# Layer 0 of a four-layer attention and GLU kernel: chunk 1 transposed by TensorE too, layer norms first, some work on GpSimd

## Chip, cores, metric

One NeuronCore of one Trainium2 chip. The metric is device time of one execution in microseconds (us), lower is better. Executions of one kernel mostly agree within 1%. Times were taken on several chips, always with runs of the kernel before on the same chip, so kernels are compared by their ratio to the kernel before.

## The reference

```python
x = x + A(layernorm(x))    # layers 0 and 2: 16 heads of 28, keys at distance 0, 2, .. 14, softmax, @ wo
x = x + B(layernorm(x))    # layers 1 and 3: h = (x @ w_gate) * (x @ w_up); h @ w_down
# x: 1 x 2048 x 448 bf16; w_gate, w_up: 448 x 1792; w_down: 1792 x 448
```

## The kernel before

Tokens are split by parity (each parity attends only to itself) and cut into 4 chunks of 512. x stays in SBUF. A chunk's path in an attention layer: layer norm on VectorE, a transpose of each normalised 128-row block into `xnTa`, QK and V matmuls, then, per query block of 120, scores, Exp, a mask product, denominators and A·V, a reciprocal as Ln and Exp, a product, and finally the `wo` matmul and the residual add. The GLU layers read the transposed `xnTb`.

The Python code contains a list scheduler. Every operation has a priority, dependencies and an assumed duration. The scheduler plays time forward with those assumed durations and so fixes, before anything runs, the order of instructions on each engine. On the chip each engine takes its instructions in that order and waits on semaphores. **A wrong assumed duration costs nothing by itself, but an instruction placed too early holds up everything behind it.**

```python
PE_T = ("00",)      # (layer, chunk) transposed by TensorE instead of by DMA
WARM = 20           # dummy matmuls at the start
SEQ = "A00 A01 B10 A02 B11 A03 B12 A20 ...".split()      # A/B, layer, chunk

    # weights of the GLU layers: issued from GpSimd once chunk 2 of x has landed
    xl = [("x", -1, 11)]
    for nm, Wt, src, ... in (("wg", WG, ...), ("wu", WU, ...)):
        plain_dma("pool", Wt[:, c, :], src[...], (nm, c), f"d_{nm}", deps=xl, lat=12000.0, prio=-30)   # ... WT likewise
    plain_dma("pool", WD[:], ..., "wd", "d_wd", deps=xl, lat=16000.0, prio=-29)
    # ...
    def ln_chunk(li, j, prio):
        # per block: bn_stats, bn_aggr (VectorE); per half or chunk: Ln, Exp (ScalarE) -> rstd
        for B in range(4 * j, 4 * j + 4):
            slot, prev = ring("xn", ...)          # 6 slots, given out in the order of ln_chunk calls;
            sc.add("dve", ... ("xn", li, B), 325.0, deps=[("rstd", li, B), ..., prev])    # prev: the slot's last transpose
            if not by_pe:
                sc.add("sp", one(lambda E: E.dma_start_transpose(X[:, :, c0:c0 + 128], xn_sb[:, slot, :]), ("T", li, B)),
                       1270.0, deps=[("xn", li, B)] + war + ..., lat=1500.0, ...)
            else:                                  # four 128x128 TensorE transposes into PSUM, one eviction by ScalarE or VectorE
    # ...
    for n, job in enumerate(SEQ):
        ln_chunk(li, j, -30.0 + n * 0.5)           # so the ring goes 00, 01, 10, 02, ...
        if job[0] == "A": a_chunk(li, j, prio)     # qk_chunk, v_group, attn_front/back, y_block
        else: b_chunk(li, j, nb, prio)
```

The softmax here doesn't subtract the row's maximum and nothing guards it: scores larger than these inputs give would overflow.

## Time and profile before

| | before |
|---|---|
| time, median (range) | 457.93 us (455.83 to 459.05) |
| span in the profile | 453.6 us |
| busy: TensorE, VectorE, ScalarE, GpSimd | 421.1, 244.1, 222.6, 11.1 us |

The median is of the three runs known before the change.

In the profile PE is TensorE's matmuls, DVE VectorE, ACT ScalarE, POOL GpSimd, SP the queue that issues the transposes; L507 is a line of the program. These are lines of the page's strip: the span in 40 slices of 11.3 us, each digit the busy share in tenths, PEclk the recorded TensorE clock in tenths of full speed.

```profile
PE   5814877999999999999999999999999999999997
PEclk9765995999999999999999999999999999999999
DMA  8896002410002210010020310020020201001001
```

From the eighth slice on TensorE is full: it bounds the kernel there. Everything to be had lies in the first seven slices. The same in numbers, from the table of windows: stretch in us, its length, then busy time (and instruction count) of PE, its weight loads, DVE, ACT and POOL, the recorded clock, the DMA share and GB/s.

```profile
24.00:39.70 15.70, 0.40 (x19) 0.26 (x18) 0.03 (x1) 2.64 (x3) 0.00 (x0) 0.58 1.04 210
39.70:44.00 4.30, 4.30 (x13) 1.06 (x13) 2.25 (x4) 0.00 (x0) 0.00 (x0) 0.54 0.30 61
44.00:68.00 24.00, 18.96 (x312) 8.37 (x311) 18.98 (x35) 21.82 (x33) 0.00 (x0) 0.99 0.01 2
68.00:78.00 10.00, 7.53 (x72) 2.97 (x71) 8.08 (x21) 4.42 (x9) 0.00 (x0) 0.51 0.27 54
78.00:453.60 375.60, 372.50 (x2713) 152.47 (x2710) 200.68 (x382) 180.80 (x281) 0.00 (x0) 1.00 0.11 23
```

TensorE did 0.40 us of work in the 15.7 us from 24 us on, while the DMA engines were full. The list of waits (who waited for whom, total us, times, longest us) names the wait:

```profile
DVE xn_sb L479 <- DMA xnTa<-xn_sb: 21.0, 1, 21.0
PE ps L507 <- DMA xnTa<-xn_sb: 15.3, 1, 15.3
```

L507 is here the QK matmul of chunk 1; L479 is a normalise, held up because its slot of the ring (the six buffers of `xn_sb`, which hold normalised blocks until they are transposed) is still being read by a transpose. The DMA queues in the window from 20 to 26 us (queue, packets, MB, share of the 16 engines) show why the transposes are late; q0 carries the weights that GpSimd issued, q1 the transposes:

```profile
q0 software_dynamic: 173, 0.96, 79.8%
q1 hardware_dynamic: 320, 0.08, 14.7%
```

The SP queue's timeline (start, length, what) has the third oddity: chunk 2's last two transposes of `xnTa` come behind four for layer 1 (`xnTb`), since the ring gives chunk (1,0) its slots before chunk (0,2).

```profile
14.58 28.02 SPq L484 DMA_TRANSPOSE xnTa<-xn_sb  x6
68.61 5.12 SPq L484 DMA_TRANSPOSE xnTb<-xn_sb  x4
77.67 2.50 SPq L484 DMA_TRANSPOSE xnTa<-xn_sb  x2
```

### The profile page before, as it was taken

Reading aid. Unit: us, or ns where it says so; the run is one execution under the profiler, and the core shown is the slowest. Engines: PE = TensorE matmul, PEld = TensorE weight load, DVE = VectorE, ACT = ScalarE, POOL = GpSimd, SP = SyncE. Lnnn points to the kernel's source line nnn. Section 1 sums busy time; section 2 is a strip of 40 time slices with the busy share of each in tenths; the row PEclk is TensorE's granted clock in tenths of the full one; section 3 lists DMA queues with packets and bytes.
Section 4 is the critical chain, followed back from the end, with each engine's and each line's share of the span. In section 5 each row is a group of like instructions: output and inputs, shape, how many; then the busy total and the mean of one; then the engine's idle time right before and its main releaser. Section 6 shows DMA issues by size and latency. Waiting matters only on the chain.

```text
span 453.6 us, 7740 instructions
## 1 busy us (share of the span) xinstructions
PE 421.1 (93%) x3204; PEld 173.1 (38%) x3204; DVE 244.1 (54%) x484; ACT 222.6 (49%) x350; POOL 11.1 (2%) x30
## 2 busy tenths in 40 slices
PE   5814877999999999999999999999999999999997
PEld 3201333333444333433344334433344334334333
DVE  6602788434769727761389616861477542442432
ACT  4530993577666567325664357434863330430330
POOL 2600000000000000000000000000000000000000
PEclk9765995999999999999999999999999999999999
DMA  8896002410002210010020310020020201001001
GB/s 283 195 227 109 2 2 57 82 26 1 0 2 49 58 36 2 0 36 12 2 48 1 69 25 1 2 47 2 0 48 32 59 0 35 7 2 40 0 2 40
DMA packets 39395, 18.63 MB, mean 41 GB/s; under 512 B 33312, under 2 KB 38448, under 8 KB 39360
## 3 DMA queue, kind: packets, MB, share of 16 engines
q1 hardware_dynamic: 37056, 11.54, 12.2%
q0 software_dynamic: 1152, 5.22, 4.6%
q10 hardware_dynamic: 1152, 1.38, 0.9%
q8 instruction: 25, 0.41, 0.4%
q14 instruction: 10, 0.08, 0.1%
HBM read 8.43 MB, written 1.84 MB: 23 GB/s over the span
## 4 chain that ended last, share of the span: by engine, by line
PE 84%; DVE 6%; DMA 6%; ACT 1%; issue 0%; SPq 0%; DVEq 0%
PE ps L507 45%; PE ps L752 19%; PE ps L519 9%; PE ps L697 5%; DMA xnTa<-xn_sb 5%; PE ps L668 2%; PE ps L645 2%; DVE st L464 2%; DMA x_sb<-in_A_x_dram 1%; PE ps L672 1%; DVE oT L683 1%; DVE E_sb L658 1%; PE ps L546 1%; DVE x_sb L702 1%; DVE xn_sb L479 1%; DVE qk L581 1%
## 5 line engine op out<-in xcount | busy, mean ns | idle before, releaser
L740 DVE TENSOR_TENSOR hT<-g_sb,ps 128x512 bf16<-128x512 bf16 x112 | 76.0, 685 | 96.4 <-ACT g_sb L737 67.4
L737 ACT ACTIVATE g_sb<-ps 128x512 bf16<-128x512 f32 x112 | 65.7, 598 | 96.6 <-PE ps L519 82.4
L507 PE MATMUL ps<-xnTb,WG 128*128 128x512 bf16 x336 | 91.3, 380 | 0.0
L507 PE MATMUL ps<-xnTb,WU 128*128 128x512 bf16 x336 | 90.9, 379 | 0.0
L752 PE MATMUL ps<-WD,hT 128*128 128x448 bf16 x448 | 90.5, 353 | 0.0
L652 ACT ACTIVATE E_sb<-ps 128x960 bf16<-128x960 f32 (+1 forms) x72 | 63.4, 926 | 43.9 <-PE ps L645 43.4
L507 PE MATMUL ps<-xnTa,WQK 128*128 128x512 bf16 x192 | 49.8, 397 | 16.7 <-DMA xnTa<-xn_sb 15.5
L702 DVE TENSOR_TENSOR x_sb<-x_sb,ps 128x448 bf16<-128x448 bf16 x64 | 39.2, 614 | 36.4 <-PE ps L752 26.2
L658 DVE TENSOR_TENSOR E_sb<-E_sb,MK 128x960 bf16<-128x960 bf16 (+1 forms) x72 | 44.8, 625 | 23.1 <-ACT E_sb L652 22.5
L752 PEld LDWEIGHTS ps<-WD,hT 128*128 128x128 bf16 x448 | 42.2, 98 | 39.2
L507 PEld LDWEIGHTS ps<-xnTb,WU 128*128 128x128 bf16 x336 | 31.6, 98 | 37.6 <-issue 0.8
L507 PEld LDWEIGHTS ps<-xnTb,WG 128*128 128x128 bf16 x336 | 26.5, 97 | 50.1 <-issue 29.1
L464 DVE BATCH_NORM_STATS2 st<-x_sb 128x6 f32<-128x448 bf16 x64 | 39.2, 619 | 4.2 <-DMA x_sb<-in_A_x_dram 3.4
L581 ACT ACTIVATE qk<-ps 128x1024 bf16<-128x1024 f32 x29 | 29.7, 1024 | 22.1 <-PE ps L519 15.0
L479 DVE TENSOR_SCALAR xn_sb<-x_sb,mv,rstd 128x512 bf16<-128x512 bf16 x64 | 22.2, 407 | 27.8 <-DMA xnTa<-xn_sb 21.0
L697 PE MATMUL ps<-wo_g,oT 128*128 128x448 bf16 x128 | 31.9, 379 | 4.4 <-DVE oT L683 4.3
L507 PEld LDWEIGHTS ps<-xnTa,WQK 128*128 128x128 bf16 x192 | 16.9, 100 | 45.3 <-issue 26.8
L519 PE MATMUL ps<-xnTb,WT 64*128 64x512 bf16 x224 | 33.9, 381 | 0.1
L677 ACT ACTIVATE R_sb<-ps 128x480 f32<-128x480 f32 (+1 forms) x36 | 19.9, 551 | 23.2 <-PE ps L668 23.2
L683 DVE TENSOR_TENSOR oT<-ps,R_sb 128x480 bf16<-128x480 f32 (+1 forms) x36 | 22.5, 626 | 15.1 <-ACT R_sb L679 11.8
L627 ACT ACTIVATE v_sb<-ps 128x896 bf16<-128x896 f32 (+1 forms) x20 | 16.8, 842 | 12.8 <-PE ps L519 12.2
L679 ACT ACTIVATE R_sb<-R_sb 128x480 f32<-128x480 f32 (+1 forms) x36 | 21.0, 583 | 0.9
(52 smaller groups left out, 192.5 us busy)
## 6 DMA issues: line engine op xcount, KB each, us to landing
x_sb<-in_A_x_dram SPq DMA_DIRECT2D x4, 448.0 KB, 7.4
out_dram<-x_sb SPq DMA_DIRECT2D x16, 112.0 KB, 1.7
WD<-in_B_w_down_dram POOLq DMA_DIRECT2D x1, 1568.0 KB, 20.9
WG<-in_B_w_gate_dram POOLq DMA_DIRECT2D x3, 448.0 KB, 4.8
WU<-in_B_w_up_dram POOLq DMA_DIRECT2D x3, 448.0 KB, 11.8
hT<-in_A_wqkv_dram ACTq DMA_DIRECT2D x4, 224.0 KB, 4.9
xnTb<-xn_sb SPq DMA_TRANSPOSE x32, 2.5
WV<-in_A_wqkv_dram ACTq DMA_DIRECT2D x4, 112.0 KB, 6.1
```

What stands on the lines that cost most here:

```text
L464: sc.add("dve", one(lambda E, B=B: E.bn_stats(st6[:, B, :], x_sb[:, B, :]), ("bn", li, B)), 525.0, deps=[("x", li - 1, B)] + ([("xn", li - ...
L507: ins.append((lambda E, u=u, c=c, st=st, sp_=sp_, which=which: E.matmul(u["out"](which), u["lhs"](which, c, 0, 128), u["rhs"](which, c, 0, ...
L519: ins.append((lambda E, u=u, c=c, lo=lo, which=which, opening=opening: E.matmul(u["out"](which), u["lhs"](which, c, lo, lo + 64), u["rhs"] ...
L581: return E.activation(dst, src, ACT.Copy) if hasattr(E, "activation") else E.tensor_copy(dst, src)
L652: return E.activation(E_sb[0:nk, slot, 2 * hp:2 * hp + 2, 0:4 * nq], ps[0:nk, b0:b0 + 2, 0:4 * nq], ACT.Exp, scale=SCALE)
L658: return E.tensor_tensor(e, e, m, ALU.mult)
L683: return E.tensor_tensor(oT[:, :, tok:tok + nq], ps[:, bk[0], 0:4 * nq].rearrange("p (h n) -> p h n", h=4), R_sb[:, rs, 0:4 * nq].rearrang ...
L697: ins.append((lambda E, hc=hc: E.matmul(ps[:, bk[0], 0:D], oT[:, hc, lo:hi], wo_g[:, hc, :], start=hc == 0, stop=hc == 3), ("Y", li, B) if ...
L702: sc.add("dve", one(lambda E: E.tensor_tensor(x_sb[:, B, :], x_sb[:, B, :], ps[:, bk[0], 0:D], ALU.add), ("x", li, B)), dve_est(D), deps=[ ...
L737: sc.add("act", one(lambda E, gs=gs, bk=bk: E.activation(g_sb[:, gs, :], ps[:, bk[0], :], ACT.Copy), ("G", li, j, fc)), act_est(512), deps ...
L740: sc.add("dve", one(lambda E, gs=gs, bk=bk, fc=fc: E.tensor_tensor(hT[:, fc, hs, :], g_sb[:, gs, :], ps[:, bk[1], :], ALU.mult), ("H", li, ...
L752: ins.append((lambda E, fc=fc, bk=bk, i=i: E.matmul(ps[:, bk[0], 0:D], hT[:, fc, hs, 128 * i:128 * i + 128], WD[:, fc, :], start=fc == 0, ...
```

## The change

The intent: take chunk 1 off the crowded DMA engines, start chunks 2 and 3 early enough to fill TensorE's bubbles, and relieve VectorE and ScalarE. Layer 0 only. The diff, cut to its core:

```diff
-PE_T = ("00",)
+PE_T = ("00", "01")
+HEAD_LN = 4        # all four layer norms of layer 0 before anything else in the ring
+POOL_MASK = 2      # second mask of a query block in chunks 0, 1 may go to GpSimd
+POOL_WQK = True    # padding of the QK weights may go to GpSimd
+LN0 = (1, 1, 2)    # chunk 0's rstd in groups of 1, 1, 2 blocks instead of 2, 2
+VFIRST = True      # for chunk 0 V at higher priority than QK
 ...
-            sc.add(("act", "dve"), one(fn, ("wqk", c, w)), ...)
+            sc.add(("act", "dve", "pool") if POOL_WQK else ("act", "dve"), one(fn, ("wqk", c, w)), ...)
 ...                     # also: bn_aggr at prio - 0.1, normalise at prio - 0.2
-                       1270.0, deps=[("xn", li, B)] + war + (["c_p0", "c_p1"] ...), ...
+                       1270.0, deps=[("xn", li, B)] + war + (["c_p0", "c_p1"] ...) + (["wd"] if li == 0 else []), ...
 ...
-            sc.add("dve", one(fm, ("E", li, qb, hp)), ...)
+            by_pool = hp == 1 and li == 0 and jh < POOL_MASK
+            sc.add(("dve", "pool") if by_pool else "dve", one(fm, ("E", li, qb, hp)), {..., "pool": 2.2 * 8 * nq}, ...)
 ...
-        ln_chunk(li, j, -30.0 + n * 0.5)
+        if n == 0:
+            for h in range(HEAD_LN):
+                ln_chunk(0, h, -30.0 + 0.5 * h)
+        if li > 0 or j >= HEAD_LN:
+            ln_chunk(li, j, -30.0 + n * 0.5)
```

The added `["wd"]` makes the remaining DMA transposes of layer 0 (chunks 2 and 3) wait until the last weight, WD, has landed.

More of the change, by code (lines that the diff above doesn't have):

```diff
@@ L429, in fn @@
                 return E.activation(dst, src, ACT.Copy) if hasattr(E, "activation") else E.tensor_copy(dst, src)
-            sc.add(("act", "dve"), one(fn, ("wqk", c, w)), {"act": 470.0, "dve": 330.0}, deps=[("stg", c), "c_wqk0"], prio=-28)
+            sc.add(("act", "dve", "pool") if POOL_WQK else ("act", "dve"), one(fn, ("wqk", c, w)), {"act": 470.0, "dve": 330.0, "pool": 600.0}, deps=[("stg", c), "c_wqk0"], prio=-28)
     WQKR = [("wqk", c, w) for c in range(4) for w in range(2)]
@@ L462, in ln_chunk @@
         X = xnT[par]
-        for B in range(4 * j, 4 * j + 4):
-            sc.add("dve", one(lambda E, B=B: E.bn_stats(st6[:, B, :], x_sb[:, B, :]), ("bn", li, B)), 525.0,
-                   deps=[("x", li - 1, B)] + ([("xn", li - 1, B)] if li else []), prio=prio)
-            sc.add("dve", one(lambda E, B=B: E.bn_aggr(mv[:, B, :], st6[:, B, :]), ("mv", li, B)), 100.0, deps=[("bn", li, B)], prio=prio)
-        halves = 2 if li == 0 and j == 0 else 1
-        by_pe = f"{li}{j}" in PE_T
-        n = 4 // halves
-        for h in range(halves):
-            B0 = 4 * j + n * h
+        by_pe = f"{li}{j}" in PE_T
+        groups = LN0 if li == 0 and j == 0 else (4,)
+        B0 = 4 * j
+        for n in groups:
+            for B in range(B0, B0 + n):
+                sc.add("dve", one(lambda E, B=B: E.bn_stats(st6[:, B, :], x_sb[:, B, :]), ("bn", li, B)), 525.0,
+                       deps=[("x", li - 1, B)] + ([("xn", li - 1, B)] if li else []), prio=prio)
+                sc.add("dve", one(lambda E, B=B: E.bn_aggr(mv[:, B, :], st6[:, B, :]), ("mv", li, B)), 100.0, deps=[("bn", li, B)], prio=prio - 0.1)
             sc.add("act", one(lambda E, B0=B0, n=n: E.activation(lnv[:, B0:B0 + n].unsqueeze(2), mv[:, B0:B0 + n, 1:2], ACT.Ln, bias=eps_sb[:, 0:1], scale=1.0), ("lnv", li, B0)),
@@ L475, in ln_chunk @@
                    165.0, deps=[("lnv", li, B0)], prio=prio)
+            B0 += n
         for B in range(4 * j, 4 * j + 4):
@@ L479, in ln_chunk @@
             sc.add("dve", one(lambda E, B=B, slot=slot, src=src: E.tensor_scalar(xn_sb[:, slot, :].rearrange("p (a n) -> p a n", a=2), src, mv[:, B, 0:1], rstd[:, B:B + 1], ALU.subtract, ALU.mult), ("xn", li, B)),
-                   325.0, deps=[("rstd", li, B), ("mv", li, B), ("x", li - 1, B), prev], prio=prio)
+                   325.0, deps=[("rstd", li, B), ("mv", li, B), ("x", li - 1, B), prev], prio=prio - 0.2)
             war = (readersA if par == 0 else readersB).get((li - 2, B), [])
@@ L484, in ln_chunk @@
                 sc.add("sp", one(lambda E, slot=slot, c0=c0: E.dma_start_transpose(X[:, :, c0:c0 + 128], xn_sb[:, slot, :]), ("T", li, B)),
-                       1270.0, deps=[("xn", li, B)] + war + ([f"c_p0", "c_p1"] if par == 0 else []), dma=f"d_t{par}_{j}", mode=li, lat=1500.0, prio=prio)
+                       1270.0, deps=[("xn", li, B)] + war + ([f"c_p0", "c_p1"] if par == 0 else []) + (["wd"] if li == 0 else []), dma=f"d_t{par}_{j}", mode=li, lat=1500.0, prio=prio)
             else:
@@ L658, in fm @@
                 return E.tensor_tensor(e, e, m, ALU.mult)
-            sc.add("dve", one(fm, ("E", li, qb, hp)), dve_est(8 * nq, 2.0, 60.0), deps=[("Ex", li, qb, hp), "c_mk"], prio=prio)
+            by_pool = hp == 1 and li == 0 and jh < POOL_MASK
+            sc.add(("dve", "pool") if by_pool else "dve", one(fm, ("E", li, qb, hp)), {"dve": dve_est(8 * nq, 2.0, 60.0), "pool": 2.2 * 8 * nq}, deps=[("Ex", li, qb, hp), "c_mk"], prio=prio)
         return slot
@@ L771, in a_chunk @@
     def a_chunk(li, j, prio):
-        qk_chunk(li, j, prio)
+        vp = prio - 0.1 if VFIRST and li == 0 and j == 0 else prio
+        if vp == prio:
+            qk_chunk(li, j, prio)
         qbs = qbs_of(j)
@@ L790, in a_chunk @@
                 rpos["v"] += 1
-            v_group(li, g, prio)
+            v_group(li, g, vp)
+        if vp != prio:
+            qk_chunk(li, j, prio)
         for qb in qbs:
```

## The prediction

> **What bounds the kernel now.** The table of windows shows two regimes. From 78 us to the end at 453.6 TensorE is busy without a gap (50.0 of 50 us per stretch) at a granted clock of 1.00: it is the bound. Before 78 us waits bind. TensorE has nothing from 24.4 to 39.7; the list of waits puts 15.3 us down to one wait of the chunk-1 QK matmuls for the DMA transposes of xn_sb. They were issued from 14.6 us and landed at 39.6: in the DMA view WG, WU, WT, WD come on the software queue from 13 to 39 us with 100% to 76% of the DMA engines, and the transposes, in packets under 512 B, got 4% to 31% until the weights were through. The Trainium skill, "DMA: Bandwidth & Descriptors", section "Queues, rings and completion order", says engines go round-robin between queues by packet; small packets against large ones would then share as seen.
>
> From 44 to 68 us ScalarE is busy 21.8 of 24, TensorE 19.0: attention of chunks 0 and 1 runs at ScalarE's pace (per query block two exps 1.83 us, Ln and Exp 1.2), with no other matmuls to fill in: chunk 2's last normalised blocks wait in a ring for layer 1's transposes (issued 77.7). At 40 to 44 and 68 to 78 the clock is 0.5 after idling. In full-clock time TensorE's work from 12.8 to 77.9 us is some 35 us (busy times clock), so 30 of 65 are lost.
>
> **What the change does.**
> - 16 TensorE transposes for chunk 1 (the first 8 took 0.72 us) and four evictions (0.59 ScalarE, 0.41 VectorE) replace the late transposes: removes the 15.3 us.
> - Chunks 2 and 3 wait for WD, which alone should land near 36 us instead of 38.9; then eight issues of 1.26 us, landing in 2.5: chunk 2 at 42, chunk 3 at 47.
> - All layer norms first: VectorE done with them by about 23 us; the ring no longer ties chunk 2 to layer 1. QK and V of chunks 2 and 3 (10 us each) and layer 1 can fill bubbles from about 40.
> - V first: WV lands at 10.5, WQK is ready at 12.7; worth up to 2 us.
> - GpSimd masks: estimate 2 to 3 us each against 0.6 on VectorE. The skill's "SBUF — State Buffer" says a VectorE instruction with two SBUF inputs contends with a GpSimd one that reads SBUF; no trace here shows it yet. Cost 0 to 3 us.
>
> **Sum.** First real matmul 10.2; half clock until 16 loses 2; bubbles from 21 to 41 lose 4 (attention from 21.5, ScalarE-bound until about 54); later 3. Work unchanged: 35 + 376 us, transposes 1, tail 3. Span 434; timed runs lie 2 to 4 above the profiled span. **Predicted 437 us, range 428 to 448.** Faster by over 2% (below 448.8): 0.92; within 2%: 0.07; slower: 0.01.
>
> **What would show it.** No wait of QK for xnTa above 3 us in layer 0; TensorE without gap from 14 to 30; attention of chunks 0 and 1 over by 55 us instead of 75; chunk-2 QK near 42 instead of 83; WD landed near 36; TensorE busy throughout from 42 at clock 1.0, with unchanged work.
>
> **What would make it wrong.** The emitted order is fixed beforehand: if WD lands late, TensorE stalls on chunk 2. If GpSimd masks block VectorE, attention becomes bound there and the bubbles return. If the clock falls to 0.5 in a sparse stretch from 30 to 42, 3 to 5 us go. If GpSimd's weight padding delays the weight loads behind it, everything after WD shifts.

## The result

The kernel after takes 433.35 us (433.00 to 433.87, 4 runs) against 456.94 us (455.83 to 459.05, 4 runs) of before: ratio 0.948, 95% interval 0.9438 to 0.9521. A ratio here is the mean time of one kernel's runs over that of the other's of the same rounds, so it is not quite the ratio of the quoted medians. Executions over 1.5% slower than the fastest of the same kernel are left out of the means. The result is correct.

| | before | after |
|---|---|---|
| span in the profile | 453.6 | 431.5 |
| TensorE busy, and span minus busy | 421.1, 32.5 | 412.2, 19.3 |
| WD landed at (issue + time to landing) | 38.9 | 32.9 |
| first chunk-1 QK after the gap / chunk 2's first QK | 39.7 / 83.0 | no gap / 48.1 |
| Ln and Exp of chunk 1's last block done | 74.9 | 66.4 |

The strip and the windows of after (slices of 10.8 us; the same stretches as far as they go):

```profile
PE   6897799999999999999999999999999999999997
PEclk9999999999999999999999999999999999999999
DMA  8794130100031200200202200010022101001001
```

```profile
24.00:39.70 15.70, 12.94 (x173) 5.56 (x175) 8.26 (x12) 13.36 (x18) 6.42 (x3) 1.00 0.68 168
39.70:44.00 4.30, 3.54 (x60) 1.60 (x56) 3.60 (x8) 3.27 (x6) 2.00 (x1) 1.00 0.31 63
44.00:68.00 24.00, 20.39 (x244) 9.05 (x243) 18.85 (x37) 17.28 (x27) 4.00 (x2) 1.00 0.22 34
68.00:78.00 10.00, 9.84 (x82) 3.93 (x82) 6.63 (x15) 6.90 (x11) 0.00 (x0) 1.00 0.20 41
78.00:431.50 353.50, 347.47 (x2544) 145.00 (x2575) 191.28 (x363) 166.97 (x263) 0.00 (x0) 1.00 0.10 22
```

The empty stretch now holds 12.94 us of TensorE work, and the two stretches at clock 0.51 to 0.54 are gone. How the 22.1 us of span divide, as an estimate from these tables: the half-clock stretches of before held 4.30 + 7.53 us of busy time at 0.54 and 0.51 (four `wo` matmuls took 1.67 us at 70.71 us, 0.92 at 60.23), so 4.30 x 0.46 + 7.53 x 0.49 = 5.7 us went to the clock; the 16 added transposes cost about 0.9 us; the rest, 22.1 - 5.7 + 0.9 = 17.3 us, is waiting that has gone. (The trace of after lacks 40 of 3220 matmul records, against none before, so its idle time is overstated by a few us and its busy time understated by as much: core_only below, with the same matmuls and no record missing, is busy 416.5 us.)

No wait of TensorE for a transposed `xnTa` is left in the list of waits. In its place are small ones, of which these are the longest in the attention stage; the last line is VectorE's longest wait in the list:

```profile
PE ps L674 <- POOL E_sb L663: 1.4, 1, 1.4
PE ps L650 <- ACT E_sb L657: 1.1, 1, 1.1
PE ps L703 <- DVE oT L689: 1.0, 1, 1.0
DVE E_sb L663 <- ACT E_sb L657: 12.0, 6, 3.3
```

The SP queue: eight transposes for chunks 2 and 3 behind WD, only then layer 1's; and in the DMA window from 20 to 26 us the weights are alone.

```profile
33.05 18.84 SPq L489 DMA_TRANSPOSE xnTa<-xn_sb  x8
54.72 20.78 SPq L489 DMA_TRANSPOSE xnTb<-xn_sb  x6
```

```profile
q0 software_dynamic: 333, 1.79, 101.4%
```

q0 moves 1.79 MB in those 6 us where it moved 0.96 MB before, although the transposes' own records fill only 14.7%; WD lands 6.0 us earlier. The loss is not simply per transpose: WD took 20.9 us from issue to landing in before and in headln_only below, whose transposes were issued from 14.6 and 14.8 us, ahead of most weight loads, but 16.0 us in pet_head, whose eight were issued from 21.5 us, and 15.1 us in core_only with none beside it. Why the early ones cost the weights more was not tested.

But V was not first. The first matmuls of after, on TensorE's timeline (idle time and what ended it in brackets):

```profile
12.48 2.74 PE L512 MATMUL ps<-xnTa,WQK 128*128 128x512 bf16 x6 [1.62 <-ACT WQK L434]
15.16 1.03 PE L524 MATMUL ps<-xnTa,WQK 64*128 64x512 bf16 x4
17.56 0.73 PE L512 MATMUL ps<-WV,xnTa 128*128 128x448 bf16 x3
```

A higher priority only decides among operations that the scheduler believes ready, and it assumes that WV takes 9.5 us from issue, where the trace of before has 6.1. So it placed QK first. Six QK matmuls in 2.74 us are also half the later rate (1.47 us for six), although the recorded clock reads 1.00 here.

GpSimd took six masks. One of them, and VectorE's two normalises beside it:

```profile
47.21 2.00 POOL L663 TENSOR_TENSOR E_sb<-E_sb,MK 128x960 bf16<-128x960 bf16 x1 [3.70 <-ACT E_sb L657]
47.71 1.97 DVE L484 TENSOR_SCALAR xn_sb<-x_sb,mv,rstd 128x512 bf16<-128x512 bf16 x2
```

Two such normalises take 0.73 us elsewhere in this trace; here 1.97, ending 0.47 us after the mask. The Trainium skill, "SBUF — State Buffer", section "Who interferes with whom", says that of GpSimd and a VectorE instruction in a two-port mode, which `tensor_scalar` can enter, the later one is blocked until the first has finished. This pair agrees with that, and it is one pair. The case that the prediction names, a VectorE instruction with two SBUF inputs, shows once, the other way round: a mask of VectorE began at 32.18 us, GpSimd's mask 0.09 us later, and that one took 2.42 us where the other five took 2.00.

```profile
32.18 0.65 DVE L663 TENSOR_TENSOR E_sb<-E_sb,MK 128x960 bf16<-128x960 bf16 x1
32.27 2.42 POOL L663 TENSOR_TENSOR E_sb<-E_sb,MK 128x960 bf16<-128x960 bf16 x1 [0.62 <-ACT E_sb L657]
```

The 2.00 us also agree with the skill's "GPSIMD Engine Reference", section "Elementwise — side-by-side cycle accounting" (about 2.6 cycles per element with two inputs, at 1.2 GHz; as an estimate from that, 960 elements take 2.08 us).

### The profile page after: what moved, and what is told of

Same layout as the page of the kernel before. It is cut to its first block, busy times and chain, and to the rows that moved or that the text cites. A ratio compares the mean times of both kernels' runs of the same rounds, so it can differ in the third digit from the quotient of the medians.

```text
span 431.5 us, 7732 instructions
## 1 busy us (share of the span) xinstructions
PE 412.2 (96%) x3180; PEld 173.9 (40%) x3220; DVE 244.3 (57%) x482; ACT 221.3 (51%) x350; POOL 24.7 (6%) x38
## 4 chain that ended last, share of the span: by engine, by line
PE 87%; ACT 5%; issue 4%; DMA 2%; DVE 1%; POOLq 0%; POOL 0%; SPq 0%; DVEq 0%
PE ps L512 47%; PE ps L758 20%; PE ps L524 9%; PE ps L703 5%; ACT E_sb L657 2%; PE ps L674 2%; PE ps L650 2%; DMA x_sb<-in_A_x_dram 2%; PE ps L678 1%; PE ps L551 1%; ACT R_sb L683 1%; ACT qk L586 0%; POOLq L831 0%; POOL E_sb L663 0%; ACT R_sb L685 0%
## 5 line engine op out<-in xcount | busy, mean ns | idle before, releaser
L512 PE MATMUL ps<-xnTb,WU 128*128 128x512 bf16 x327 | 89.5, 379 | 1.1 <-issue 0.6
L512 PE MATMUL ps<-xnTb,WG 128*128 128x512 bf16 x313 | 86.4, 380 | 2.9 <-issue 1.4
L663 DVE TENSOR_TENSOR E_sb<-E_sb,MK 128x960 bf16<-128x960 bf16 (+1 forms) x66 | 41.0, 625 | 29.8 <-ACT E_sb L657 29.4
L512 PE MATMUL ps<-xnTa,WQK 128*128 128x512 bf16 x184 | 46.6, 390 | 3.0 <-ACT WQK L434 1.6
L703 PE MATMUL ps<-wo_g,oT 128*128 128x448 bf16 x128 | 28.9, 353 | 1.1 <-DVE oT L689 1.0
L484 DVE TENSOR_SCALAR xn_sb<-x_sb,mv,rstd 128x512 bf16<-128x512 bf16 x64 | 23.5, 426 | 2.8 <-ACT rstd L478 2.7
L512 PE MATMUL ps<-WV,xnTa 128*128 128x448 bf16 x96 | 21.4, 353 | 0.9 <-ACT E_sb L657 0.8
L632 ACT ACTIVATE v_sb<-ps 128x896 bf16<-128x896 f32 (+1 forms) x17 | 14.8, 873 | 13.5 <-PE ps L524 13.1
```

Source lines behind the costliest of these rows:

```text
L512: ins.append((lambda E, u=u, c=c, st=st, sp_=sp_, which=which: E.matmul(u["out"](which), u["lhs"](which, c, 0, 128), u["rhs"](which, c, 0, ...
L663: return E.tensor_tensor(e, e, m, ALU.mult)
L703: ins.append((lambda E, hc=hc: E.matmul(ps[:, bk[0], 0:D], oT[:, hc, lo:hi], wo_g[:, hc, :], start=hc == 0, stop=hc == 3), ("Y", li, B) if ...
```

## The experiments

Theory A: the gain is the removed wait of chunk 1's QK for transposes that starved beside the weight loads, plus bubbles filled by chunks 2 and 3. Rivals: the ring order alone (B), the small parts (C, D), transposes by DMA being slow of themselves (E). All kernels are built from one file with every part of the change behind a constant; with all parts off it emits exactly the order of before, with all on that of after. All results were correct. "core" means `PE_T` and `HEAD_LN` as after and the wait for WD, the rest as before.

| run | ratio to before (95%) | median us | before, same chip |
|---|---|---|---|
| pet_only | 0.9657 (0.9639 to 0.9675) | 440.66 | 456.26 |
| headln_only | 0.9837 (0.9818 to 0.9855) | 448.73 | 456.26 |
| core_only | 0.9474 (0.9457 to 0.9490) | 432.18 | 456.26 |
| no_pool_mask | 0.9507 (0.9489 to 0.9524) | 433.92 | 456.26 |
| weights_wait | 0.9612 (0.9584 to 0.9639) | 438.76 | 456.76 |
| pet_head | 0.9615 (0.9587 to 0.9644) | 439.12 | 456.76 |
| vfirst_core | 0.9464 (0.9439 to 0.9489) | 432.11 | 456.76 |
| warm_core | 0.9463 (0.9438 to 0.9488) | 431.89 | 456.76 |
| pet_head_lat | 0.9509 (0.9457 to 0.9562) | 432.95 | 455.87 |
| late15_pe0 | 0.9500 (0.9463 to 0.9537) | 432.35 | 455.87 |
| late15_pe01 | 0.9477 (0.9436 to 0.9517) | 431.36 | 455.87 |
| pe_012_core | 0.9528 (0.9490 to 0.9567) | 433.72 | 455.87 |

### pet_only: TensorE transposes for chunk 1, nothing else

```diff
-PE_T = ("00",)
+PE_T = ("00", "01")
```

> The kernel before with one thing changed: chunk 1 of layer 0 is also transposed by TensorE. Theory A (the gain is mostly the removed wait of chunk-1 QK for its DMA transposes; the layer-norm order only fills bubbles): about 441 us (437 to 445), no TensorE gap of over 3 us between 13 and 40 us, WD landing near 33 instead of 38.9, chunk-2 QK still late (after 60 us). Theory B (the gain is mostly the untied ring, which lets chunk 2 in early): 450 us or more.

440.66 us, as theory A has it: 15.6 us of the 24 come from this line. WD landed at 33.5. Chunk 2's QK came at 67.9, and the clock was down again before that:

```profile
48.00:56.00 8.00, 5.42 (x84) 2.15 (x78) 7.34 (x17) 6.21 (x12) 0.00 (x0) 0.64 0.16 33
56.00:64.00 8.00, 6.94 (x55) 2.83 (x54) 5.62 (x13) 1.86 (x4) 0.00 (x0) 0.51 0.29 55
```

### headln_only: layer norms first, nothing else

```diff
+HEAD_LN = 4        # PE_T = ("00",), no wait for WD
```

> The kernel before with only the order changed: all four layer norms of layer 0 first, chunks 1 to 3 still by DMA transposes, which do not wait for WD. Theory A: no gain, 452 to 460 us, because twelve transposes instead of six now share the engines with the weights; the chunk-1 QK wait stays near 15 us or grows. Theory B: 445 us or less.

448.73 us: neither theory. The wait stayed, as A said:

```profile
PE ps L514 <- DMA xnTa<-xn_sb: 14.3, 1, 14.3
```

But 7.5 us were gained all the same, because after the wait chunk 2's QK ran from 52.6 us instead of 83.0 and helped to fill TensorE: in the windows from 40 to 72 us it was busy 29.0 of 32 us, in before 25.6. The first of those matmuls:

```profile
52.64 0.81 PE L514 MATMUL ps<-xnTa,WQK 128*128 128x512 bf16 x3
```

I had taken the order for worthless alone; it is worth about half of what the transposes are, at another place. The two gains, 15.6 and 7.5 us, add up to 23.1, near the 24.1 of core_only. But core_only has the wait for WD as well: the two edits by themselves are pet_head below, and gain 17.6 us.

### core_only: both, with the wait for WD

```diff
+PE_T = ("00", "01"); HEAD_LN = 4; deps of the layer-0 DMA transposes + ["wd"]
-POOL_MASK = 2, POOL_WQK = True, LN0 = (1, 1, 2), VFIRST = True, prio - 0.1, prio - 0.2
```

> TensorE transposes for chunk 1, layer norms first, chunks 2 and 3 waiting for WD; without GpSimd masks, GpSimd weight padding, the 1-1-2 grouping, V first and the small priority changes. Theory A: these four small parts are worth under 2 us together, so 431 to 436 us. Rival C: they are worth 4 us or more together: 437 or more.

432.18 us, ratio 0.9474 against 0.948 of after. The four small parts and the two priorities together are not to be told from nothing.

### no_pool_mask: the kernel after without GpSimd masks

```diff
-POOL_MASK = 2
+POOL_MASK = 0
```

> The kernel after with all masks on VectorE. Theory A (the GpSimd masks, 2.0 us each against 0.65, lengthen the chain and once hold up VectorE, which was not short of time): 430 to 433 us, TensorE's waits of 1.4 and 1.0 us for GpSimd gone. Rival D (they relieve VectorE): 435 us or more.

433.92 us, ratio 0.9507; its interval overlaps that of after. Neither the gain that I expected nor rival D's loss: the masks moved to GpSimd are worth nothing that these runs resolve, although both the waits for GpSimd and the blocked normalises are in the trace of after. Why they cost so little was not tested. Against core_only, which ran on the same chip in the same rounds, this kernel is 1.7 us slower (433.21 to 434.48 us against 432.07 to 433.07): what it has more, the padding on GpSimd, the grouping, V first and the priorities, does not help and may cost a little.

### weights_wait: the kernel before with the weight loads behind chunk 1's transposes

```diff
-    xl = [("x", -1, 11)]
+    xl = [("x", -1, 11), ("T", 0, 7)]
```

> The kernel before with one dependency more: the loads of wo, WG, WU, WT and WD wait until chunk 1's DMA transposes have landed. TensorE transposes none but chunk 0, as before. Theory A (contention: the transposes were slow only because the weight loads held the DMA engines): chunk 1's transposes land near 21 us instead of 39.6, the 15.3 us wait of chunk-1 QK falls to 2 us or less, total 438 to 444 us, like the kernel where TensorE transposes chunk 1 (440.7). Rival E (DMA transposes are slow of themselves at this point): they land after 30 us and the total stays above 448.

438.76 us with no more TensorE transposes than before: rival E falls. The DMA timeline of GpSimd shows when the last of chunk 1's transposes was through, since GpSimd waits for it:

```profile
22.24 2.53 POOL L394 DMA_DIRECT2D wo_g<-in_A_wo_dram  x4 [18.53 <-DVE xn_sb L486]
```

So 22.2 us instead of 39.6 (the releaser in brackets is the last normalise by the profile; what the instruction waits on is the transposes' semaphore). No wait of TensorE for `xnTa` is in this run's list. The transposes were late only because of the weights. The Trainium skill, "DMA: Bandwidth & Descriptors", section "Queues, rings and completion order", says that each DMA engine goes round-robin between queues by packet. The trace of before fits this only loosely: between 20 and 26 us q1 got 320 packets through and q0 173, between 26 and 32 us 257 and 258. But q1's packets were small, 0.08 MB in all in the first of these stretches, where its share was 14.7%.

### pet_head: core without the wait for WD

```diff
-deps of the layer-0 DMA transposes + ["wd"]
```

> core_only (432.2 us) without the wait of chunks 2 and 3 for WD, so their eight DMA transposes are issued among the weight loads. Theory A: they starve until the weights are through and land near 40 us, where core_only has them at 37 to 43, and WD lands later, near 38, when nothing needs it yet: 431 to 435 us, so the wait for WD is worth 2 us at most. Rival F (the wait is what makes the early order pay): 437 us or more.

439.12 us. My expectation was wrong, rival F right: the one dependency is worth 1.4% (0.9615 against 0.9474). Yet the transposes did better by the clock: the last was issued at 37.4 us, in core_only at 48.6. VectorE shows the loss:

```profile
35.74 0.74 DVE L486 TENSOR_SCALAR xn_sb<-x_sb,mv,rstd 128x512 bf16<-128x512 bf16 x2 [6.43 <-DMA xnTa<-xn_sb]
36.39 1.79 DVE L665 TENSOR_TENSOR E_sb<-E_sb,MK 128x960 bf16<-128x960 bf16 x3
37.09 0.59 PE L676 MATMUL ps<-E_sb,ones 128*32 128x480 bf16 x4 [6.07 <-DVE E_sb L665]
```

Chunk 3's last two normalises need ring slots that chunk 2's starving transposes still read. The scheduler assumed that these land in 1.5 us, so it put the normalises ahead of three masks; VectorE sat 6.43 us, and TensorE 6.07 us behind the masks.

### pet_head_lat: the same DMAs, another assumption

```diff
-                       ..., mode=li, lat=1500.0, prio=prio)
+                       ..., mode=li, lat=1500.0 if li or j < 2 else 12000.0, prio=prio)
```

> pet_head (439.1 us) again without the wait for WD; only the number that the kernel's own scheduler assumes for the landing of chunk 2's and 3's transposes is raised from 1.5 to 12 us, so the emitted order changes and the DMAs do not. In pet_head VectorE, in order, sat 6.4 us before a normalise of chunk 3 that waited for a ring slot. Theory H (the wait for WD pays only because it puts the late landing into the emitted order): 431 to 434 us, no VectorE wait above 2 us for these transposes. Theory I (the traffic itself costs): stays at 437 or more.

Theory H holds: 432.95 us (three fast runs, 432.62 to 433.18), with no wait for WD. A changed number in the scheduler's table, which no DMA sees, gives back what dropping the wait had lost. So the wait for WD pays through the emitted order, not through quieter DMA engines. The profile of this kernel fell in an execution of 1046.02 us (see the last section), so its VectorE waits at full speed were not seen. The order can be read even there: chunk 3's last two normalises come after eight masks, in pet_head after one. And its first transposes still went out among the weights, from 26.1 us, where WD landed at 33.2.

### vfirst_core: V really first

```diff
+VFIRST = True; assumed landing of WV 9500 -> 6000 ns
+        tdeps = ... + (["c_p0", "c_p1"] if li == 0 else [])     # V reads the zeroed padding
```

> core_only (432.2 us) with V really emitted first on TensorE for chunk 0 (in the kernel after, V first was asked for but QK still came first in TensorE's order). The prediction's step: V begins near 10.7 us instead of QK at 12.8, worth up to 2 us, so 430 to 431.5. Rival G: attention starts when QK of chunk 0 is evicted, which V first delays by its own time, and TensorE is at half rate there; no gain or a loss, 432 to 435.

432.11 us, ratio 0.9464: nothing to tell from core_only, so rival G. V began at 11.69 us, but at half rate:

```profile
11.69 2.45 PE L515 MATMUL ps<-WV,xnTa 128*128 128x448 bf16 x6
14.45 1.31 PE L515 MATMUL ps<-WV,xnTa 128*128 128x448 bf16 x6
```

The first scores came at 25.29 us, in core_only at 24.75. (The first build lacked the second line of the diff: V read padding columns with no wait for their zeroing. In after the order happens to cover this.)

### warm_core: keep TensorE busy before the first QK

```diff
-WARM = 20
+WARM = 40      # and ten more dummy matmuls after chunk 0's transposes
```

> core_only (432.2 us) with 20 more dummy matmuls at the start and 10 after chunk 0's transposes, so that TensorE is hardly idle before the first QK. Theory: the first QK group (six matmuls in 2.74 us, against 1.47 us later) runs at half rate because TensorE idled before; kept busy, it takes about 1.5 us and the kernel gains 1.5 to 2.5 us: 429.5 to 431. Rival: the half rate has nothing to do with idling, or the start is bound elsewhere: 432 or more.

431.89 us, ratio 0.9463: no gain that can be told. The dummies did not do their work: five QK matmuls still took 2.13 us, and the dummies pushed QK from 12.81 to 13.24 us. Whether idling is the cause of the half rate stays open; this filling was not enough.

### late15_pe0 and late15_pe01: chunks 1 to 3, or 2 and 3, by DMA before the weights

```diff
-    ... WG, WU, WT, WD: deps=xl
+    wl = xl + [("T", 0, 15)]
+    ... WG, WU, WT, WD: deps=wl          # layer-0 transposes do not wait for WD
-PE_T = ("00", "01")                      # late15_pe0 only
+PE_T = ("00",)
```

> Layer norms first, but only chunk 0 on TensorE as in the kernel before: all twelve other transposes of layer 0 by DMA, and WG, WU, WT and WD wait for the last of them; wo loads early. Theory A (contention with the weights was the only trouble): chunk 1 lands near 21 us, chunk 3 near 31, WD near 47, nothing waits for them: 429 to 433 us, as good as or better than TensorE transposes. Rival: WG and WU come too late for layer 1, or chunk 1 is later than by TensorE: 434 or more.

> As late15_pe0, but chunks 0 and 1 on TensorE: core_only (432.2 us) with the order of the DMAs turned round, chunks 2 and 3 before the weights. Chunk 2's QK can then begin before 35 us instead of 47 and fill the bubbles of 24 to 56 us, of which core_only has about 4 us: 428.5 to 431. If the bubbles are not for want of matmuls to run but come from the order: 432 or more.

Ratios 0.9500 and 0.9477, in the same band as core_only. late15_pe0 is where theory A put it; the 431.36 us of late15_pe01 fall between the two ranges of its expectation. With the DMAs in this order no further TensorE transposes are needed at all. In late15_pe01 chunk 2's matmuls did fill the stretch from 24 to 40 us (15.34 us busy against 14.03 in core_only), but TensorE ran dry later. Windows of core_only, then of late15_pe01:

```profile
24.00:40.00 16.00, 14.03 (x193) 5.67 (x191) 12.21 (x20) 13.85 (x18) 0.00 (x0) 1.00 0.70 162
56.00:64.00 8.00, 8.00 (x57) 3.07 (x55) 4.76 (x12) 5.28 (x9) 0.00 (x0) 1.00 0.20 33
```

```profile
24.00:40.00 16.00, 15.34 (x169) 6.41 (x171) 12.01 (x20) 11.84 (x18) 5.45 (x9) 1.00 0.60 150
56.00:64.00 8.00, 6.40 (x99) 2.99 (x102) 5.73 (x12) 6.01 (x10) 0.00 (x0) 1.00 0.36 67
```

The filler was only spent sooner: from 24 to 80 us TensorE is busy 51.97 us in core_only and 51.99 in late15_pe01. (The trace of late15_pe01 lacks some records here, 585 matmuls to 594 weight loads, so it may be busy a us or so more; the times show no gain.) Layer 1 cannot start before the attention of chunk 0 is through, and in late15_pe01 TensorE waits 1.40 us for `xnTb` at 62.3 us.

### pe_012_core: chunk 2 on TensorE too

```diff
+PE_T = ("00", "01", "02")
```

> core_only (432.2 us) with chunk 2 on TensorE too. Chunk 2's QK is free from about 27 us instead of 47. It adds 16 transposes (about 1 us) and four evictions of 0.4 to 0.6 us on VectorE and ScalarE, which pace this stage: 429.5 to 432 if the filling wins, 433 or more if the evictions do.

433.72 us, ratio 0.9528, in the range where I had said that the evictions win, though its interval overlaps core_only's. That the evictions are the cause is not shown: its first scores came at 27.34 us, in core_only at 24.75, and TensorE waited 1.3 us for `xnTb`. No version beat core_only beyond the intervals, so the simplest, core_only, is what I would keep.

## Why the prediction was right

The time lay inside the range, 3.7 us below the forecast of 437, and the main mechanism was shown: pet_only and weights_wait remove the starved transposes in two different ways and gain 15.6 and 18.0 us of medians; headln_only shows the filling of bubbles on its own, 7.5 us. Step by step:

- "removes the 15.3 us": right, 15.6 us alone.
- "QK and V of chunks 2 and 3 ... can fill bubbles from about 40": right in kind; chunk 2's QK came at 48.1, not 42. Its four transposes, issued from 33.05 to 36.98 us and landing in 2.5 to 4.3 us, were through by about 41, so they were not what it waited for.
- "VectorE done with them by about 23 us": wrong. Chunk 3's last two normalises need ring slots that chunk 2's transposes read, and these wait for WD; they ran at 47.71 us.
- "WD ... near 36": wrong by 3 us; 32.9. I had charged the weights only with the transposes' own share of the engines, and q0 moved nearly twice as much without them between 20 and 26 us.
- "First real matmul 10.2" and "V first; worth up to 2 us": wrong. The scheduler did not emit V first, and vfirst_core shows that it is worth nothing.
- "attention from 21.5, ScalarE-bound until about 54": wrong. First scores at 26.9, Ln and Exp over at 66.4; ScalarE was busy 31.6 of the 39.5 us between, so it had time to spare. It probably mattered little because TensorE had other work: it was busy 32.4 us of the same stretch.
- "bubbles from 21 to 41 lose 4 ... later 3": TensorE idled 2.8 us from 24 to 39.7 and 4.5 us from 39.7 to 78 (0.76 + 3.61 + 0.16), some of it missing records. About right.
- GpSimd masks, "2 to 3 us each", "Cost 0 to 3": 2.00 us, one 2.42; no effect on the time that the runs resolve.
- The mis-sized terms: the sum (434.2 us of span; 431.5 were measured) counts the tail of 3 us twice, once by itself and once in the 376 us from 78 us to the end. The first matmul came 2.3 us late, so these two nearly cancel, which is luck. The work was sized right, by an estimate from core_only, whose trace is complete: 410.1 us busy from its first QK on, where the sum has 35 + 372.5 + 1 + 2 = 410.5 (372.5 are the busy part of the 376). So the 2 us or so that are left lie in the bubbles, part of whose measured length is missing records. And the step from span to timed run was taken as 3 us, where it was 1.8 (433.28 and 431.5), which is 1.2 of the 3.7 us.
- A part that the prediction did not price: the wait for WD. It was listed as a delay; it is worth 1.4%, through the emitted order (pet_head, pet_head_lat).

## What to carry to other kernels

A small DMA that something waits for should not share the engines with a bulk load that nobody needs yet: here, moving it to TensorE and putting the bulk load behind it gained about the same (15.6 and 18.0 us). In a kernel whose order is fixed beforehand, an honest assumed latency can be worth as much as the wait that keeps the transfers apart (pet_head_lat), because one instruction that waits in order holds up all behind it. Once TensorE was nearly full, handing it filler earlier only moved the bubble, and neither relief for VectorE and ScalarE nor an earlier start of V was worth anything that these runs resolve.

## What the Trainium skill lacked or had wrong

- "DMA: Bandwidth & Descriptors", section "Rules for kernel authors", says that a transpose next to ordinary DMAs needs nothing. That speaks of correctness; for time it lacks a warning. Chunk 1's four transposes took 20.8 us from issue to landing (median) beside the weights, and 2.5 us without them in weights_wait; and WD took 20.9 us to land with them beside it from the start, 15.1 us without.
- "TensorE: Matmul & The Clock Gate", section "Seeing it yourself", warns that recorded clock events can be unreliable. The runs agree: after's record reads 1.00 while six QK matmuls took 2.74 us against 1.47 later, and in before the same 2.74 us stand at a recorded 0.5.
- No page clearly has this: one of four executions of pet_head_lat took 1046.02 us at a recorded clock of 1.00, with the WD matmuls at 752 ns each against 353 in after. Its other three runs took 433 us. The same warning mentions a clock seen stuck low for over 50 us; whether this was such a case is open.
